# Pairing the small transforms on TensorE, moving a buffer and a store, and sending weights out earlier, in a two-layer convolution and FFN kernel

## The chip, the cores and the metric

The kernel runs on one core of one Trainium2 chip. Its time is the device time of one execution in microseconds (us). Before the change the median of three runs is 916.47 us (916.46 to 917.86). The engines are named as in the profile: PE is TensorE (matrix multiply), DVE is VectorE, ACT is ScalarE, POOL is GpSimd, SP is SyncE, which here only issues DMA transfers. PSUM is the memory that PE writes to; DVE and ACT empty it.

## The reference

Two layers follow each other; each adds a gated long convolution and then a gated FFN to x (2048 tokens, 576 features, 4608 hidden features). All inputs are bf16.

```python
def _A_ref(q, k, v, shift_k, ssm_k, ssm_D):
    ...                                   # k_shift: 4 taps along the tokens
    kv = k_shift * v
    kv_f = rfft(kv padded to 2*S); kf_f = rfft(ssm_k padded to 2*S)
    y = irfft(kv_f * kf_f)[:S]            # causal convolution, by feature
    y = y + kv * ssm_D
    return q * y
def _B_ref(x, w_gate, w_up, w_down):
    return (_gelu(x @ w_gate) * (x @ w_up)) @ w_down
x = A_q
x = x + _A_ref(_layernorm(x), A_k, A_v, A_shift_k, A_ssm_k, A_ssm_D)
x = x + _B_ref(_layernorm(x), B_w_gate, B_w_up, B_w_down)
...                                       # the same two lines once more
```

The convolution of a layer does not depend on x, so its result y serves both layers; only the factor q*y and the FFN follow each other.

## The kernel before, in words

**Tokens and visits.** The tokens are four chunks of 512. A unit is (layer, chunk): in order (0,0), (0,1), (1,0), (1,1), then the same for chunks 2 and 3. The hidden features are split in three phases of 1536. A visit is one unit with one phase; there are 24 visits, 1 to 3 for the first unit, then 4 to 9 for the next two in turn, and so on. Units are numbered from 0, so visit 4 is the first visit of unit 1, which is chunk 1 of layer 0.

**A visit on PE.** First 12 feature tiles (`gu`, line 1047). Each is 18 matmuls: nine steps, in each of which a matmul for w_gate uses rows 0 to 63 of the array and one for w_up rows 64 to 127, at the same time. Their result lies in one PSUM buffer of 2 x 512 columns. Then the down matmuls (`dn`, line 1643), which use all 128 rows: four token blocks of 24 matmuls with 288 columns.

**PSUM.** There are four buffers. One belongs to the convolution (`cps`); three serve feature tiles and down sums in turn (`pr`), so feature tile n+3 can only start when tile n has been read out. In the first visits ("hurry", until the inverse transform of chunk 1 is placed) ACT reads a tile out by a Gelu (line 1614) and a copy (line 1615), and DVE multiplies the two halves (line 1616). Later ACT does the Gelu (line 1624) and DVE multiplies straight out of PSUM (line 1625), so that PSUM is freed by DVE. The scratch tiles `ga` of this have two buffers, which the squares for the layer norm (`junk`, lines 868 and 887) use too.

**The small transforms.** The convolution is made by blocks of 512 tokens from small transforms on PE: for chunk 1 `fwd_eo` (line 299), 8 steps of 4 matmuls for the filter and 8 for kv; for chunks 2 and 3 `quarter` (line 310), 2 matmuls each; and the inverse (line 352), 4 steps of 4 matmuls for each chunk. ACT copies each forward result out of PSUM (`eo`, lines 302 and 312), DVE makes sums and differences from it (`cross`, line 317), and the products follow on DVE. The products of shifted k and v (`kvt`, lines 253 and 259) are DVE's too.

**Rows.** To bring a unit to its FFN: ACT makes the gate factor `yh` (line 921, two buffers), DVE multiplies (line 931), POOL makes the mean, ACT the sum of squares (line 887), POOL the root, DVE the norm (`xn`, line 960). Four such rows of 128 tokens make up a chunk. SP transposes each into `xnT` by two DMA transposes (line 1002); every feature tile of a visit reads all four. `xnT` has two buffers.

**What sets the order.** The program is written out once, engine by engine. A planner (`Pace`) carries estimated clocks for PE, DVE and ACT; `fill` is called after every feature tile and down step and puts in what it reckons to be ready, and `run_p` puts in a small transform. The engines run their lists in order, so a mistaken estimate shows as a wait. Weights are loaded on SP: `weights` issues a load that falls due within 30 us, or within HOLD = 14 us as long as rows are pending. A group of feature weights is three loads (lines 820 to 822).

**Other names in the change.** `hh` is the filter's spectrum for chunk 1, before in two `kc` tiles and a `y` tile (`hh_tiles`). `natural` transposes filter blocks 2 and 3 by DMA and stores them to DRAM (lines 1128 and 1129, both on SP). `conv.alt` lets a small transform borrow one of the three turning PSUM buffers; before, that is so only in the down part of a visit.

Of the kernel before, what the change touches and what calls it, by code (L numbers as in the profile page):

```python
# [17 lines left out]
P = 128  # L18
# [3 lines left out]
RT = BS // P  # L22
# [13 lines left out]
C_HB = 0.345  # L36
C_FOLD = 0.38
LAG = 0.25
AHEAD = 2.0
SLOW, PRESS = 6.0, 22.0  # L40
HOLD, SOON, QUIET, LEAD, FAR = 14.0, 30.0, 10.0, 1.8, 3.6

# [90 lines left out]
class Conv:  # L133
# [8 lines left out]

    def __init__(self, tc, ctx, pace, gwork, A_k, A_v, A_shift_k, A_ssm_k, A_ssm_D, ident, cps, ypool):
# [34 lines left out]
        self.quiet = 0.0  # L178
        self.eo_at = {"eo": deque([0.0] * 2), "yh": deque([0.0] * 2)}
        self.U, self.gwork = deque(), gwork  # L180
# [187 lines left out]

    def hh_tiles(self, kt):
        if kt == 0:  # L370
            for k in (0, 2):
                self.hh[k] = self.kcp.tile([P, 2, self.D], BF16, tag="kc", name="hh")[:]
        else:
            self.y[1] = self.ypool.tile([P, RT, self.D], BF16, tag="y", name="y")
            for k in (1, 3):
                self.hh[k] = self.y[1][:, k - 1:k + 1, :]

    def step(self, m, kv=None, loaded=False):
# [74 lines left out]
        def fwd(kt, s, h):  # L453
            def run():
                if s == 0 and h == 0:
                    for k in (kt, kt + 2):
                        kc[k] = self.kcp.tile([P, 2, D], BF16, tag="kc", name="kc")
                if (kt, s, h) == (1, 0, 0):
                    self.flush(NEVER)
                free, ring = self.eo_free(True)  # L460
# [20 lines left out]
        def fwd_h(kt, s, h):  # L481
            def run():
                if s == 0 and h == 0:
                    self.hh_tiles(kt)
                free, ring = self.eo_free(True)
# [24 lines left out]
        def v(kt, a, part):  # L510
            def run():
# [6 lines left out]
                def fin(when):  # L518
                    if part == 1:
                        if m == 1 and (kt, a) == (2, 0):  # L520
                            mark("early", when)
# [135 lines left out]
        def steps(filt, ready):  # L657
# [7 lines left out]
            for kt in range(2):  # L665
                for s in range(2):
                    for h in range(2):
                        self.Pq.append((lambda now=filt or kt == 0: max(
                            ready(), 0.0 if self.eo_at["eo"] or self.eo_at["yh"] else NEVER,
                            0.0 if now or "early" in at else NEVER), 0.49, (fwd_h if filt else fwd)(kt, s, h)))  # L670
        steps(True, get("h"))
# [26 lines left out]
    def run_v(self, limit):  # L698
# [15 lines left out]
        return True  # L714

    def run_p(self):
        t = self.t
# [3 lines left out]
        self.cur = 0 if self.ps_free[0] <= t.pe else 1  # L721
        if self.cur and ready() <= t.pe and self.ps_free[0] <= t.pe + (0.0 if (1, RT - 1) in self.y_at else 0.3):
            self.cur = 0
            t.pe = max(t.pe, self.ps_free[0])
# [3 lines left out]
        run()  # L728
        t.pe += cost
        return True  # L730

@with_exitstack
def ssm_geglu_kernel(ctx, tc, A_q, A_k, A_v, A_shift_k, A_ssm_k, A_ssm_D, B_x, B_w_gate, B_w_up,
# [39 lines left out]
    def other():  # L773
        b = pr("cps")
        bank_at[taken[0] % 3] = 0.0
        return b

# [10 lines left out]

    bank_at = [0.0] * 3

    def pr(name):
        while late and taken[0] - late[0][1] >= 2:
            add_late()
        taken[0] += 1
        bank_at[taken[0] % 3] = NEVER
        return bank(turn[(taken[0] - 1) % 3], name)
# [10 lines left out]
    work = pool("work", 2)  # L807
    conv = Conv(tc, ctx, t, gwork, A_k, A_v, A_shift_k, A_ssm_k, A_ssm_D, ident,
                lambda *form: bank(turn[3], "cps", *form), ypool)
# [245 lines left out]
    def turn_row(ui, j, xn, when, entry):  # L1055
# [18 lines left out]
        xn_done[ui] = j + 1  # L1074

    conv.alt_at = lambda: bank_at[(taken[0] + 1) % 3]
    early = {}
# [6 lines left out]
    def weights():  # L1084

        while due:
# [15 lines left out]

    def fill(limit, tensor, conv_first):
        weights()
# [17 lines left out]
    nat = []  # L1122

    def natural(b):
# [3 lines left out]
        nc.sync.dma_start_transpose(out=h, in_=A_ssm_k[:, b * BS:(b + 1) * BS])  # L1128
        nc.sync.dma_start(out=conv.hs[b].rearrange("(r p) d -> p r d", p=P), in_=h)

    with tc.manual_schedule():
# [432 lines left out]
        for at, (wb, ph, ui, first, final) in enumerate(visits):  # L1564
# [30 lines left out]
            hT = hpool.tile([P, FP, CH], BF16, tag="hT", name="hT")  # L1595
            free, gone = deque([0.0] * 3), deque([0.0] * 2, maxlen=2)
            conv.alt = None
            for fi in range(FP):
                n, gi = divmod(wb * FP + fi, FG)
                w = wgu[n]  # L1600
                if wb == 0 and fi in early:
                    pair = early.pop(fi)
                    taken[0] += 1
                    gu_half(pair, fi, 1)
                    t.pe = max(t.pe, free.popleft()) + C_GU / 2
                else:
                    pair = pr("gu")
                    gu(pair, w, gi, lambda a: a, xnT)
                    t.pe = max(t.pe, free.popleft()) + C_GU
                while run_late(NEVER):  # L1610
                    pass
                if (hurry() or conv.V and not aq) and t.act <= t.pe + 0.2:
# [5 lines left out]
                    gone.append(t.on_dve(C_HB, there + 0.15) + 0.1)  # L1618
                    free.append(there + 0.1)
                    bank_at[taken[0] % 3] = free[-1]  # L1620
                    lead = FAR
                else:
# [3 lines left out]
                    gone.append(t.on_dve(C_HT, t.on_act(C_GELU, max(t.pe + 0.15, gone[0])) + 0.15) + 0.1)  # L1626
                    free.append(gone[-1])
                    bank_at[taken[0] % 3] = free[-1]
# [5 lines left out]
                fill(t.pe + C_GU + (lead if fi < FP - 2 else LEAD), hurry(), conv.left > 0)  # L1634
            ahead[:] = [t.pe + RT * FP * C_DN, visits[at + 1][2] if at + 1 < len(visits) else None]
            for j in range(RT):
                acc = pr("dn")
                conv.alt = other
                xa = x_c[c][:, j, :]
# [24 lines left out]
                if layer == 1 and end:  # L1664
# [7 lines left out]
                    else:  # L1672
                        conv.store(dst, ob, t.pe + 0.2 + C_EVD + LAG, entry)
                    bank_at[taken[0] % 3] = t.on_dve(C_EVD, t.pe + 0.2) + 0.15
                else:
                    def plus(c=c, j=j, layer=layer, ph=ph, end=end, acc=acc, xa=xa, xh=xh):
# [11 lines left out]
                        if layer == 0 and end:  # L1688
                            vq.extend(prep(units.index((1, c)), j))
                    late.append((t.pe + 0.2, taken[0], plus))  # L1690
        conv.flush(NEVER)
# [50 lines left out]
```

## Time and profile before

| | us |
|---|---|
| median of 3 runs | 916.47 |
| the profiled execution, its own time | 916.75 |
| its span | 915.0 |
| first feature tile starts | 40.29 |
| visit 2 starts | 85.75 |
| visit 3 starts | 121.03 |
| visit 4 starts | 160.91 |
| PE busy | 910.2 |
| DVE busy | 559.1 |
| ACT busy | 364.0 |
| POOL busy | 139.1 |

The profile is of one execution. Its own time is 1.75 us above its span and 0.28 us above the median of the runs. Busy PE time counts a matmul from start to end, and matmuls overlap, so PE's load is better read from the distance between starts. In the lines of the timeline the columns are: start, length, engine, line, operation, what it writes and reads, how many of them; in brackets the idle time before and what ended it.

### The profile page before, as it was taken

The page shows a single profiled execution, that of the slowest core. Times are in us where ns is not written, and L with a number is a line of the kernel's source. Part 1 is how long each engine was busy: PE and PEld are TensorE (multiplying, and loading weights), DVE is VectorE, ACT ScalarE, POOL GpSimd, SP SyncE. Part 2 cuts the span into 40 slices and gives each one's busy share as a digit, 9 for nine tenths or more (in the row PEclk, how much of TensorE's full clock was granted, in tenths as well). Part 3 has the DMA queues.
Part 4 walks back from the last instruction along what each step waited for, and adds up shares of the span by engine and source line. Part 5 has one row for each costly group of instructions (what it writes and reads, how often), then busy time and mean ns, then how long its engine had stood idle before and what let it go on. Part 6 is the DMA issues. An engine that isn't in the chain of part 4 may idle for free.

```text
span 915.0 us, 19143 instructions
## 1 busy us (share of the span) xinstructions
PE 910.2 (99%) x8049; PEld 520.9 (57%) x8049; DVE 559.1 (61%) x1111; ACT 364.0 (40%) x677; POOL 139.1 (15%) x310
## 2 busy tenths in 40 slices
PE   9999999999999999999999999999999999999998
PEld 7746556465565564655655655646646546556555
DVE  8897989644889886568887843553332334433332
ACT  7774437525435366254244233441121224321211
POOL 5422003320113012231023001210000002100000
PEclk9999999999999999999999999999999999999999
DMA  9999996968519503996944700791720820778640
GB/s 238 313 269 197 241 208 106 194 221 156 182 53 232 138 1 42 273 155 165 247 143 94 161 22 27 132 168 50 146 78 2 155 79 14 143 171 179 131 104 27
DMA packets 128635, 129.40 MB, mean 141 GB/s; under 512 B 43298, under 2 KB 120995, under 8 KB 128548
## 3 DMA queue, kind: packets, MB, share of 16 engines
q1 hardware_dynamic: 119666, 93.81, 49.7%
q0 software_dynamic: 8736, 33.77, 12.1%
q8 instruction: 63, 1.03, 0.5%
q10 hardware_dynamic: 146, 0.59, 0.2%
q14 instruction: 24, 0.20, 0.1%
HBM read 106.91 MB, written 11.80 MB: 130 GB/s over the span
## 4 chain that ended last, share of the span: by engine, by line
PE 99%; POOL 0%; ACT 0%; DVE 0%; issue 0%; ACTq 0%
PE gu L1047 61%; PE dn L1643 31%; PE ps L282 1%; PE cps L299 1%; PE cps L310 1%; PE cps L352 1%; PE ps L1268 0%; PE ps L1047 0%; PE ps L1403 0%; POOL rstd L1488 0%; PE ps L1181 0%; PE ps L1239 0%; PE ps L276 0%; ACT yh L1450 0%; PE ps L1297 0%; POOL ve L1487 0%
## 5 line engine op out<-in xcount | busy, mean ns | idle before, releaser
L1047 PE MATMUL gu<-xnT,wgu 64*128 64x512 bf16 x5148 | 561.8, 376 | 0.0
L1047 PEld LDWEIGHTS <-wgu 64*128 64x128 bf16 x5220 | 250.9, 94 | 305.8 <-issue 8.3
L1643 PE MATMUL dn<-wd,hT 128*128 128x288 bf16 x2304 | 292.8, 286 | 0.0
L1643 PEld LDWEIGHTS <-hT 128*128 128x128 bf16 x2304 | 223.6, 98 | 65.4 <-issue 8.1
L1625 DVE TENSOR_TENSOR hT<-ga,gu 128x512 bf16<-128x512 f32 x173 | 118.7, 687 | 177.1 <-ACT ga L1624 176.8
L1624 ACT ACTIVATE ga<-gu 128x512 f32<-128x512 f32 x173 | 103.0, 596 | 311.4 <-PE gu L1047 309.4
L1614 ACT ACTIVATE ga<-gu 128x512 bf16<-128x512 f32 x113 | 67.5, 598 | 164.7 <-PE gu L1047 155.1
L1616 DVE TENSOR_TENSOR hT<-ga 128x512 bf16<-128x512 bf16 x114 | 47.8, 421 | 60.4 <-ACT ga L1615 60.3
L1615 ACT CAST ga<-gu 128x512 bf16<-128x512 f32 x113 | 65.5, 580 | 0.0
L879 POOL TENSOR_SCALAR means<-s 128x1 f32<-128x1 f32 x28 | 8.5, 304 | 230.7 <-DVE x_c L1679 212.1
L1685 DVE SCALAR_TENSOR_TENSOR x_c<-dn,means,x_c 128x576 f32<-128x576 f32 x28 | 22.9, 816 | 30.2 <-PE dn L1643 30.2
L1687 DVE TENSOR_TENSOR x_c<-x_c,dn 128x576 f32<-128x576 f32 x32 | 24.1, 752 | 26.0 <-PE dn L1643 25.7
L895 POOL TENSOR_TENSOR rstd<-ve,neghalf_t 128x1 f32<-128x1 f32 x56 | 33.2, 593 | 4.7
L329 DVE TENSOR_TENSOR prod<-prod 128x576 bf16<-128x576 bf16 x64 | 29.3, 458 | 2.2
L312 ACT ACTIVATE eo<-cps 128x576 f32<-128x576 f32 x32 | 20.6, 654 | 21.2 <-DVE ab L317 7.0
L1666 DVE TENSOR_TENSOR xn<-x_c,dn 128x576 bf16<-128x576 f32 x15 | 11.3, 754 | 27.6 <-PE dn L1643 27.6
L638 DVE TENSOR_TENSOR kc<-ab,cd 128x288 bf16<-128x288 f32 x64 | 25.3, 452 | 0.0
L921 ACT ACTIVATE yh<-y,rstd 128x576 f32<-128x576 bf16 x28 | 21.3, 772 | 8.3 <-DVE x_c L931 6.3
L427 POOL DMA_DIRECT2D kr<-Kd x20 | 11.1, 554 | 85.4 <-DVE prod L328 83.7
L879 POOL TENSOR_SCALAR nm<-s 128x1 f32<-128x1 f32 x28 | 9.0, 320 | 94.2 <-DVE x_c L931 94.1
L887 ACT ACTIVATE junk<-x_c,nm 128x576 bf16<-128x576 f32 x28 | 21.6, 770 | 1.8 <-DVE hT L1625 1.1
L432 POOL DMA_DIRECT2D hr<-Hd x32 | 17.4, 545 | 28.4 <-DVE prod L328 26.4
(179 smaller groups left out, 607.8 us busy)
## 6 DMA issues: line engine op xcount, KB each, us to landing
wgu<-in_B_w_gate_dram SPq DMA_DIRECT2D x45, 576.0 KB, 5.9
wd<-in_B_w_down_dram SPq DMA_DIRECT2D x30, 864.0 KB, 6.9
wgu<-in_B_w_up_dram SPq DMA_DIRECT2D x45, 512.0 KB, 7.7
hr<-Hd POOLq DMA_DIRECT2D x32, 288.0 KB, 6.3
kr<-Kd POOLq DMA_DIRECT2D x24, 288.0 KB, 5.2
Kd<-kc POOLq DMA_DIRECT2D x12, 288.0 KB, 7.2
k<-in_A_k_dram POOLq DMA_DIRECT2D x3, 1008.0 KB, 11.2
wgu<-in_B_w_up_dram SPq DMA_DIRECT2D x45, 64.0 KB, 7.5
```

Of the source, the lines that this page charges most:

```text
L329: nc.vector.tensor_tensor(out=dst[:, cols], in0=pr[:, 0, cols], in1=pr[:, 1, cols], op=ALU.subtract if part == 0 else ALU.add)
L638: nc.vector.tensor_tensor(out=into[k][:, plane, cols], in0=a, in1=b, op=op)
L895: nc.gpsimd.tensor_tensor(out=v["rstd"][:], in0=ve[:], in1=neghalf_t[:, 0:1], op=ALU.pow)
L1047: nc.tensor.matmul(cols(pair[:, s, :]), lhsT=w[r0:r0 + HK, k, gi * P:(gi + 1) * P], rhs=cols(xnT[r0:r0 + HK, blk_of[k], :]), start=(k == 0 ...
L1614: nc.scalar.activation(out=ga[:, 0, :], in_=pair[:, 0, :], func=ACT.Gelu_apprx_tanh)
L1615: nc.scalar.copy(out=ga[:, 1, :], in_=pair[:, 1, :])
L1616: nc.vector.tensor_tensor(out=hT[:, fi, :], in0=ga[:, 0, :], in1=ga[:, 1, :], op=ALU.mult)
L1624: nc.scalar.activation(out=ga[:], in_=pair[:, 0, :], func=ACT.Gelu_apprx_tanh)
L1625: nc.vector.tensor_tensor(out=hT[:, fi, :], in0=ga[:], in1=pair[:, 1, :], op=ALU.mult)
L1643: nc.tensor.matmul(acc[:, h, 0:HW], lhsT=hT[:, fi, j * P:(j + 1) * P], rhs=wd[2 * wb + fi // WT][:, fi % WT, h * HW:(h + 1) * HW], start=( ...
L1685: nc.vector.scalar_tensor_tensor(out=xh, in0=acc[:, :, 0:HW], scalar=m_[:, 0:1], in1=xh, op0=op, op1=ALU.add)
L1687: nc.vector.tensor_tensor(out=xh, in0=xh, in1=acc[:, :, 0:HW], op=ALU.add)
```

## The change

1. A forward or inverse transform may now be placed between feature tiles only if the next one can follow it at once, into a borrowed PSUM buffer (`pair_ready`), or if it has been passed over more than twice; and, until the inverse of chunk 1 is placed, only if DVE is reckoned to run out of work before the feature tiles of the visit end (`dry`, or if the folded sums for chunk 1's inverse are made). `conv.alt` is therefore set between feature tiles too. Among down matmuls transforms go in as before.
2. The planner keeps account of the borrowed buffer (`borrowed`, `was`) and adds 0.2 us for each place with transforms between feature tiles (`C_TURN`).
3. `hh` becomes one tile in the `xnT` buffers; with that the flush of spills and the "early" condition go.
4. The store of filter block 3 moves from SP to POOL and is issued 22 us after its transpose (`NAT`, `puts`).
5. HOLD goes from 14 to 18 us.

```diff
+C_TURN = 0.2
...
+NAT = 22.0
+HOLD, SOON, QUIET, LEAD, FAR = 18.0, 30.0, 10.0, 1.8, 3.6
...
+    def hh_tiles(self):
+        t = self.xtp.tile([P, RT, 2, self.D], BF16, tag="xnT", name="hh")
+        for k in range(RT):
+            self.hh[k] = t[:, k, :, :]
...
+    def dry(self, tiles):
+        t = self.t
+        work = sum(u[1] for u in self.U) + tiles * C_HB
+        for ready, cost, _ in self.V:
+            if ready() > t.pe:
+                break
+            work += cost
+        return max(t.dve, t.pe) + work < t.pe + tiles * C_GU
+
+    def pair_ready(self):
+        t = self.t
+        if not self.Pq or self.Pq[0][0]() > t.pe:
+            return False
+        two = (len(self.Pq) > 1 and self.Pq[1][0]() <= t.pe and len(self.eo_at["eo"]) + len(self.eo_at["yh"]) > 1
+               and self.ps_free[0] <= t.pe + 0.3 and self.alt is not None and self.alt_at() <= t.pe)
+        self.skipped = 0 if two else self.skipped + 1
+        return two or self.skipped > 2
...
     def weights():
-
+        while puts and puts[0][0] <= t.pe:
+            puts.popleft()[1]()
         while due:
...
+        conv.between = between is not None
+        if tensor and between is not None and not ((1 in conv.z_at or conv.dry(between)) and conv.pair_ready()):
+            return
...
-        nc.sync.dma_start(out=conv.hs[b].rearrange("(r p) d -> p r d", p=P), in_=h)
+
+        def put():
+            (nc.sync if b == 2 else nc.gpsimd).dma_start(out=conv.hs[b].rearrange("(r p) d -> p r d", p=P), in_=h)
+        if b == 2:
+            put()
+        else:
+            puts.append((t.pe + NAT, put))
...
-                    t.pe = max(t.pe, free.popleft()) + C_GU
+                    t.pe = max(t.pe, was[0]) + C_GU
...
+                conv.alt = other if hurry() and not early else None
+                before = t.pe
+                fill(t.pe + C_GU + (lead if fi < FP - 2 else LEAD), hurry(), conv.left > 0, FP - 1 - fi)
+                if t.pe > before:
+                    t.pe += C_TURN
```

More of the change, by code (lines that the diff above doesn't have):

```diff
@@ L40 @@
 SLOW, PRESS = 6.0, 22.0
-HOLD, SOON, QUIET, LEAD, FAR = 14.0, 30.0, 10.0, 1.8, 3.6
+NAT = 22.0
+HOLD, SOON, QUIET, LEAD, FAR = 18.0, 30.0, 10.0, 1.8, 3.6
 class Pace:
@@ L133, with __init__ @@
 class Conv:
-    def __init__(self, tc, ctx, pace, gwork, A_k, A_v, A_shift_k, A_ssm_k, A_ssm_D, ident, cps, ypool):
+    def __init__(self, tc, ctx, pace, gwork, xtp, A_k, A_v, A_shift_k, A_ssm_k, A_ssm_D, ident, cps, ypool):
         self.tc, self.nc, self.t = tc, tc.nc, pace
@@ L177, in __init__ @@
         self.ps_free, self.cur, self.alt, self.alt_at = [0.0, 0.0], 0, None, None
-        self.quiet = 0.0
+        self.quiet, self.skipped, self.between = 0.0, 0, False
         self.eo_at = {"eo": deque([0.0] * 2), "yh": deque([0.0] * 2)}
-        self.U, self.gwork = deque(), gwork
+        self.U, self.gwork, self.xtp = deque(), gwork, xtp
         self.kr_free, self.hr_free = [0.0] * 3, [0.0] * 4
@@ L367, in flush @@
             self.spills.popleft()[1]()
[L369 to L376, printed above, removed]
+    def hh_tiles(self):
+        t = self.xtp.tile([P, RT, 2, self.D], BF16, tag="xnT", name="hh")
+        for k in range(RT):
+            self.hh[k] = t[:, k, :, :]
     def step(self, m, kv=None, loaded=False):
@@ L482, in run @@
             def run():
-                if s == 0 and h == 0:
-                    self.hh_tiles(kt)
+                if (kt, s, h) == (0, 0, 0):
+                    self.hh_tiles()
                 free, ring = self.eo_free(True)
@@ L519, in fin @@
                     if part == 1:
-                        if m == 1 and (kt, a) == (2, 0):
-                            mark("early", when)
                         if m == 1:
@@ L667, in steps @@
                     for h in range(2):
-                        self.Pq.append((lambda now=filt or kt == 0: max(
-                            ready(), 0.0 if self.eo_at["eo"] or self.eo_at["yh"] else NEVER,
-                            0.0 if now or "early" in at else NEVER), 0.49, (fwd_h if filt else fwd)(kt, s, h)))
+                        self.Pq.append((lambda: max(
+                            ready(), 0.0 if self.eo_at["eo"] or self.eo_at["yh"] else NEVER), 0.49, (fwd_h if filt else fwd)(kt, s, h)))
         steps(True, get("h"))
@@ L721, in run_p @@
         self.cur = 0 if self.ps_free[0] <= t.pe else 1
-        if self.cur and ready() <= t.pe and self.ps_free[0] <= t.pe + (0.0 if (1, RT - 1) in self.y_at else 0.3):
+        if self.cur and ready() <= t.pe and self.ps_free[0] <= t.pe + (0.3 if self.between else 0.0):
             self.cur = 0
@@ L729, in run_p @@
         t.pe += cost
+        if self.cur:
+            self.borrowed(self.ps_free[1])
         return True
@@ L773, in other @@
     def other():
-        b = pr("cps")
-        bank_at[taken[0] % 3] = 0.0
-        return b
+        return pr("cps")
     def run_late(limit):
@@ L787, in add_late @@
         bank_at[n % 3] = t.on_dve(C_EVD, ready) + 0.15
-    bank_at = [0.0] * 3
+    bank_at, was = [0.0] * 3, [0.0]
     def pr(name):
@@ L794, in pr @@
         taken[0] += 1
+        was[0] = bank_at[taken[0] % 3]
         bank_at[taken[0] % 3] = NEVER
@@ L1074, in turn_row @@
         xn_done[ui] = j + 1
+    conv.borrowed = lambda when: bank_at.__setitem__(taken[0] % 3, when)
     conv.alt_at = lambda: bank_at[(taken[0] + 1) % 3]
@@ L1101, in pressing, with fill @@
                 and t.pe > due_at[0] - PRESS)
-    def fill(limit, tensor, conv_first):
+    def fill(limit, tensor, conv_first, between=None):
         weights()
@@ L1120, in fill @@
                     break
-    nat = []
+    nat, puts = [], deque()
     def natural(b):
@@ L1595, in ssm_geglu_kernel @@
             hT = hpool.tile([P, FP, CH], BF16, tag="hT", name="hT")
[L1596 removed]
+            gone = deque([0.0] * 2, maxlen=2)
             conv.alt = None
@@ L1604, in ssm_geglu_kernel @@
                     gu_half(pair, fi, 1)
-                    t.pe = max(t.pe, free.popleft()) + C_GU / 2
+                    t.pe += C_GU / 2
                 else:
@@ L1618, in ssm_geglu_kernel @@
                     gone.append(t.on_dve(C_HB, there + 0.15) + 0.1)
-                    free.append(there + 0.1)
-                    bank_at[taken[0] % 3] = free[-1]
+                    bank_at[taken[0] % 3] = there + 0.1
                     lead = FAR
@@ L1637, in ssm_geglu_kernel @@
                 acc = pr("dn")
+                mine = taken[0]
                 conv.alt = other
@@ L1689, in plus @@
                             vq.extend(prep(units.index((1, c)), j))
-                    late.append((t.pe + 0.2, taken[0], plus))
+                    late.append((t.pe + 0.2, mine, plus))
         conv.flush(NEVER)
```

10 lines of the change are left out of this document (3 added, 7 removed).

## The prediction

> **What bounds the kernel now.** I read the page first: busy times and the chain of waits that ended last.
>
> ```profile
> PE 910.2 (99%) x8049; PEld 520.9 (57%) x8049; DVE 559.1 (61%) x1111; ACT 364.0 (40%) x677; POOL 139.1 (15%) x310
> PE 99%; POOL 0%; ACT 0%; DVE 0%; issue 0%; ACTq 0%
> ```
>
> PE sets the end, and the view of waits has no wait of PE after the first feature tile (40.29 us; two of 0.17 and 0.07 show only in the distance of starts). So the change can gain only by sparing PE work or gaps between its matmuls, and loses by any new wait of PE. Next the timeline of PE, in visit 3, where the inverse transforms stand singly between feature tiles:
>
> ```profile
> 132.15 2.12 PE L1047 MATMUL gu<-xnT,wgu 64*128 64x512 bf16 x18
> 134.20 0.66 PE L352 MATMUL cps<-yb,V 128*128 128x288 bf16 x4
> 134.79 2.12 PE L1047 MATMUL gu<-xnT,wgu 64*128 64x512 bf16 x18
> ...
> 137.44 9.89 PE L1047 MATMUL gu<-xnT,wgu 64*128 64x512 bf16 x90
> 147.26 2.87 PE L1643 MATMUL dn<-wd,hT 128*128 128x288 bf16 x22
> ```
>
> One tile and one transform take 134.79 - 132.15 = 2.64. A plain tile is 1.94 (five take 9.82, less a switch, over 5). Four matmuls of 288 columns are 4 x 0.1225 = 0.49 (28 down matmuls from 156.40 to 159.83). What is left, 0.21, is the price of going from 64-row to 128-row matmuls and back.
>
> How near the other engines are is in the stretches and timelines. Busy us of PE, PEld, DVE, ACT in a stretch:
>
> ```profile
> 45.00:71.00 26.00, 26.00 (x220) 11.02 (x219) 24.05 (x49) 20.76 (x44) 7.50 (x16) 1.00 1.05 246
> ```
>
> DVE is 92% busy in visit 1's feature tiles. Then the timelines of DVE, ACT and SP as the rows of unit 1 are made, towards visit 4:
>
> ```profile
> 137.10 0.76 DVE L253 TENSOR_TENSOR kvt<-k,skc 128x1152 bf16<-128x1152 bf16 x1
> 138.11 0.81 DVE L931 SCALAR_TENSOR_TENSOR x_c<-x_b,means,yh 128x576 f32<-128x576 bf16 x1
> 140.65 0.68 DVE L1625 TENSOR_TENSOR hT<-ga,gu 128x512 bf16<-128x512 f32 x1
> ```
> ```profile
> 139.60 0.60 ACT L1624 ACTIVATE ga<-gu 128x512 f32<-128x512 f32 x1 [0.36 <-PE gu L1047]
> 140.09 0.77 ACT L921 ACTIVATE yh<-y,rstd 128x576 f32<-128x576 bf16 x1
> ```
> ```profile
> 145.59 12.54 SPq L1002 DMA_TRANSPOSE xnT<-xn  x8
> 158.67 0.63 SPq L820 DMA_DIRECT2D wgu<-in_B_w_gate_dram  x1
> ```
>
> Eight transposes, then weights. The last transpose is issued at 156.87 and lands 3.4 later, at 160.24; visit 4 starts at 160.91. That is only 0.67 of room. Last, a case with weights before a chunk's last row, on SP:
>
> ```profile
> 582.97 0.63 SPq L820 DMA_DIRECT2D wgu<-in_B_w_gate_dram  x1
> 583.65 0.63 SPq L821 DMA_DIRECT2D wgu<-in_B_w_up_dram  x1
> 584.33 0.64 SPq L822 DMA_DIRECT2D wgu<-in_B_w_up_dram  x1
> 585.07 2.61 SPq L1002 DMA_TRANSPOSE xnT<-xn  x2
> ```
> ```profile
> DMA to landing us min/median/max: 2.5/7.0/7.7
> ```
>
> Those two transposes took 7.0 and 7.7 to land, where 2.5 is the least.
>
> **The change part by part.** The sum is made against the profiled execution (span 915.0, time 916.75), 0.28 above the median of the runs.
>
> *Switches.* The built programs have the same matmuls in another order. Before, transforms stand between feature tiles 15 times (11 in visit 1, the last just before the down matmuls, and 4 in visit 3); after, 6 times (4 and 2). Counting changes from 64-row to 128-row matmuls: 38 before, 30 after. 8 x 0.21 = -1.7. Among down matmuls a transform costs no switch. The ends are 0 and -1.7: no more can be saved by this.
>
> *Visit 1, ACT behind.* A pair gives DVE one product (0.33 from start to start), four sums (4 x 0.37) and two kvt operations (0.67 and 0.79): 3.26. The tile, the pair and a switch give it 1.94 + 0.98 + 0.21 = 3.13. After the fourth pair two tiles follow with the same 3.26 against 1.94 each, so DVE falls some 3 behind, of which about 1 is room; the Gelu two tiles on wants a `ga` buffer that a late product holds, so ACT is about 2 late. From there each tile costs ACT 0.49 + 0.47 + 0.76 (Gelu, copy, square) = 1.72 of 1.94, so in four to five tiles it regains 1 and reads out the last tile about 1.2 late. The first `eo` copy after it (0.65) ends 0.38 + 1.2 + 0.49 + 0.47 + 0.65 + 0.05 = 3.2 after the last feature matmul starts; the third transform, which wants that PSUM buffer, is due after 0.31 + 2 x 0.1225 + 0.98 + 6 x 0.1225 = 2.3. So PE waits 1.0. Before, this part has one wait of 0.17 among down matmuls (starts 77.28 and 77.57 against a pitch of 0.12). Ends: 0.2 and 1.5.
>
> The Trainium skill (TensorEngine Tiling (Array Packing), section PSUM Bottleneck) says that packing speeds up TensorE but not the reading out of PSUM, which may then bound. If reading out stayed hidden, switches and this part would come to -1.7; by the page's rule to less than that, and the rows of ACT above, which give -0.7, agree with it.
>
> *Visit 3, a ring of waits.* In the new order ACT's list has two gate factors (line 921) each ahead of a tile's Gelu that is already due. Each needs a `yh` buffer that DVE's gate step (line 931) frees; that step stands behind the previous tile's product. Before, a Gelu stood ahead of such a factor (139.60, then 140.09). One turn: 0.81 (931) + 0.09 + 0.67 (921, start to start) + 0.60 (1624) + 0.03 + 0.60 (1625) = 2.80 against 1.94, so 0.86 of wait; two turns, +1.7. The first hangs on DVE being late by kvt work as at 137.10. Ends: 0.9 and 1.9.
>
> *Rows behind weights (visit 4).* On SP the new order is rows 1 to 3, a group of weights, row 4. PE is at this point later by -1.7 + 1.0 + 1.7 = +1.0, and one square (0.77) more stands ahead of the Gelu that row 1's norm follows. Row 1's transposes: 145.59 + 1.0 + 0.8 = 147.4. Six issues of 1.25 make 7.5, so the weights go out at 154.9. In the three cases in which weights stand just ahead of a chunk's last row, its second transpose landed 11.4, 11.1 and 9.5 after the group's first issue (363.83 to 375.24, 582.97 to 594.08, 780.36 to 789.86), 10.7 on average. So row 4 is there at 165.6. PE is ready at 160.91 + 1.0 = 161.9 and waits 3.7. Lower end: without the square and with 9.5, 1.7; upper: 0.6 later on ACT and 11.4, 5.0.
>
> The Trainium skill (DMA: Bandwidth & Descriptors, section Queues, rings and completion order) says that a DMA engine takes descriptors in ring order, but that completion is not in order of issue. By ring order the sum below stands; if row 4 overtook the weights, it would be 917.5.
>
> *Other weights (HOLD).* For units 3 and 5 the group now goes out ahead of an earlier row, so row 4 is no longer behind it. Those landings (375.24, 594.08) were just in time for visits 10 (378.73) and 16 (594.35): no gain, and no wait seen to lose.
>
> *The store.* SP no longer waits for the transposed load, which lands at 85.48. PE waited for no weights there, so no gain. POOL takes one issue and waits for that landing; its next load came at 95.29 before. Cost 0, hidden by 9 us; with no cover it would delay that load by what the landing is late.
>
> *hh.* Its buffer was last read by PE before 40 us, and unit 1's `xnT` follows it long after its products. 0 either way: the visit-1 wait above is counted with ACT.
>
> Sum: -1.7 + 1.0 + 1.7 + 3.7 = **+4.7**: span 919.7, time 921.4, and against the median 916.47 + 4.7 = **921.2**.
>
> **The rivals.**
>
> - *Row 4 isn't held by the weights.* It lands 2.5 after its last issue (158.1), at 160.7, before PE. Then -1.7 + 1.0 + 1.7 = +1.0: 917.5, not slower beyond the measurement. It decides where the landing is less than 7 after the weights' issue. Against it: three of three cases. For it: at 780.36 it was 9.5.
> - *ACT and DVE keep up.* Neither wait of visits 1 and 3 arises; PE is at visit 4 at 159.2, the weights go out at 152.2 and row 4 lands at 162.9: wait 3.7, sum +2.0: 918.5. For it: before, PE lost but 0.25 in all to such waits. Against: the lists above, added by rows.
> - *Only the switches count.* Neither, and row 4 on time: 914.8. Against it all of the above.
>
> **How the numbers follow.** Chances: forecast 0.69, row 4 not held 0.12, engines keep up 0.10, switches only 0.09. About 0.2% (1.8 us) is what can be told from no change: above 918.3 is slower, below 914.6 faster. The third case lies on the bound, 0.06 slower and 0.04 same; the last is split 0.05 faster, 0.04 same. So slower 0.75, same 0.20, faster 0.05. Range: the forecast's own is 917.6 (all lower ends: -1.7 + 0.2 + 0.9 + 1.7 = +1.1) to 923.2 (all upper: -1.7 + 1.5 + 1.9 + 5.0 = +6.7); with the second and third cases 917.0 to 923.2, which leaves out the last and some tails.
>
> **What would show it.** In the changed kernel: 30 switches of 0.21; a PE gap of about 1 at the third transform among visit 1's down matmuls, on ACT; two of 0.86 in visit 3's feature tiles, on DVE's product; visit 4 starting at about 165.6 after a wait on row 4's transposes, which land 7 to 8 after issue; nothing later. Wrong if row 4 lands some 3 after issue, or if ACT reads out visit 1's last tile at once.

## The result and the profile after

The changed kernel takes 923.46 us (median of 6 runs, 922.74 to 924.12) against 916.47 in the same session (916.46 to 918.76): +7.0 us between the medians, where +4.7 was forecast. By the means of all these runs it is 1.0070 times as long, 95% interval 1.0057 to 1.0083. Its profiled execution took 923.76, with a span of 921.9 against 915.0.

Lines of the changed kernel are 2 to 28 higher than before: `fwd_eo` 299 is now 301 and the `eo` copy 302 is 304, `gu` 1047 is 1061, `dn` 1643 is 1671, the early Gelu and copy 1614 and 1615 are 1639 and 1640 and their product 1616 is 1641, the single Gelu 1624 is 1648, its product 1625 is 1649, the squares 887 are 901, the gate factor 921 is 935, the gate step 931 is 945, the row transposes 1002 are 1016, the weights 820 to 822 are 834 to 836.

The page of the changed kernel, busy times and the chain that ended last:

```profile
PE 910.2 (99%) x8049; PEld 524.0 (57%) x8049; DVE 558.3 (61%) x1111; ACT 362.9 (39%) x676; POOL 141.5 (15%) x311
PE 91%; DVE 5%; ACT 2%; DMA 1%; issue 1%; POOL 1%; SPq 0%; ACTq 0%; DVEq 0%
```

PE's busy time is what it was. The chain is no longer PE's alone. What PE waited for, in us, times, longest:

```profile
PE gu L1061 <- DMA wgu<-in_B_w_up_dram: 4.6, 1, 4.6
PE gu L1061 <- DVE hT L1649: 1.4, 2, 0.7
...
PE cps L301 <- ACT eo L304: 0.9, 1, 0.9
```

These are the three places that were forecast: visit 4, visit 3, visit 1. The first is put down to a weight load, but visit 4 begins with a group that had gone out at 129.58. The wait is for several semaphores; which one counts is settled by the first experiment. The view counts idle time from a modelled end; the distance between starts, less the usual pitch, gives 4.895 - 0.216 = 4.68, twice 0.86, and 1.177 - 0.1225 = 1.05.

Visit 1: PE's timeline at the third transform among the down matmuls, then ACT's ahead of it (`junk` is a square).

```profile
71.29 0.65 PE L301 MATMUL cps<-v,T 128*128 128x288 bf16 x4 [0.89 <-ACT eo L304]
```
```profile
62.70 0.60 ACT L1639 ACTIVATE ga<-gu 128x512 bf16<-128x512 f32 x1 [1.55 <-DVE hT L1641]
...
69.48 0.25 ACT L901 ACTIVATION_READ_ACCUMULATOR junk<-x_b,means 128x1 f32 x1
69.57 0.64 ACT L1639 ACTIVATE ga<-gu 128x512 bf16<-128x512 f32 x1
70.05 0.64 ACT L1640 CAST ga<-gu 128x512 bf16<-128x512 f32 x1
70.51 1.27 ACT L304 ACTIVATE eo<-cps 128x576 f32<-128x576 f32 x2
```

The Gelu at 62.70 waits 1.55 for a late product of DVE. From there a Gelu, a copy and a square take ACT 1.72 for each tile, so it gains little on PE's 1.94. It reads out the last feature tile only after another square, and the first `eo` copy ends 2.9 after the down matmuls began at 68.27.

Visit 3: PE, then ACT, then DVE.

```profile
139.19 2.12 PE L1061 MATMUL gu<-xnT,wgu 64*128 64x512 bf16 x18 [0.69 <-DVE hT L1649]
142.03 6.00 PE L1061 MATMUL gu<-xnT,wgu 64*128 64x512 bf16 x54 [0.71 <-DVE hT L1649]
```
```profile
137.16 0.78 ACT L935 ACTIVATE yh<-y,rstd 128x576 f32<-128x576 bf16 x1 [3.18 <-DVE x_c L945]
137.84 0.58 ACT L1648 ACTIVATE ga<-gu 128x512 f32<-128x512 f32 x1
140.00 0.78 ACT L935 ACTIVATE yh<-y,rstd 128x576 f32<-128x576 bf16 x1 [1.57 <-DVE x_c L945]
```
```profile
138.46 0.69 DVE L1649 TENSOR_TENSOR hT<-ga,gu 128x512 bf16<-128x512 f32 x1 [1.41 <-ACT ga L1648]
139.06 0.81 DVE L945 SCALAR_TENSOR_TENSOR x_c<-x_b,means,yh 128x576 f32<-128x576 bf16 x1
141.29 0.69 DVE L1649 TENSOR_TENSOR hT<-ga,gu 128x512 bf16<-128x512 f32 x1 [1.41 <-ACT ga L1648]
```

The ring can be read off: the factor waits for the gate step (line 945), the Gelu stands behind the factor, the product waits for the Gelu, the next gate step stands behind the product. One turn is 140.00 - 137.16 = 2.84, where a tile takes 1.94.

Visit 4: SP's queue, and how long the second of the last two transposes (159.20) took to land; the trace has no landing of the first.

```profile
147.63 7.81 SPq L1016 DMA_TRANSPOSE xnT<-xn  x6
155.53 0.60 SPq L834 DMA_DIRECT2D wgu<-in_B_w_gate_dram  x1
...
157.93 3.04 SPq L1016 DMA_TRANSPOSE xnT<-xn  x2
```
```profile
DMA to landing us min/median/max: 7.3/7.3/7.3
```

Row 4 is complete at 159.20 + 7.34 = 166.54, 11.0 after the weights' first issue. Up to here the forecast holds. But visit 4 is also longer than before, 37.37 against 35.53, although it has only two transform matmuls (0.245) more. The stretches around its start show why (busy us of PE, PEld, DVE, ACT, POOL, then the granted clock of PE as a share of full speed):

```profile
161.00:166.00 5.00, 0.39 (x6) 0.11 (x3) 2.31 (x7) 0.39 (x2) 2.46 (x5) 0.97 1.28 153
166.00:169.00 3.00, 3.00 (x14) 1.16 (x16) 0.00 (x0) 0.00 (x0) 0.00 (x0) 0.50 1.11 188
169.00:170.00 1.00, 1.00 (x12) 0.47 (x10) 0.00 (x0) 0.21 (x1) 0.00 (x0) 0.96 1.15 222
```

For some 3 us after the wait, PE runs at half clock: a step of two feature matmuls starts every 0.43 us and not every 0.216. No term of the forecast had this.

The balance of the two spans, by distances between starts: switches 8 x 0.21 = -1.7; visit 1 +0.9 (the wait of 1.05 and others of 0.06, less 0.2 of before); visit 3 +1.65; wait at visit 4 +4.7; a second short wait there, on row 4's second transpose, +0.4; half clock +1.2; first feature tile 0.26 sooner, -0.25. The sum is +6.9, which is the difference of the spans. The last item is not the change's: two later runs of before's instruction order started at 40.03 too. From visit 5 on all visits are as long as before.

### The profile page after: what moved, and what is told of

The parts are those of the page before. It is cut to its first block, busy times and chain, and to the rows that moved or that the text cites. A ratio compares the mean times of both kernels' runs of the same rounds, so it can differ in the third digit from the quotient of the medians.

```text
span 921.9 us, 19147 instructions
## 1 busy us (share of the span) xinstructions
PE 910.2 (99%) x8049; PEld 524.0 (57%) x8049; DVE 558.3 (61%) x1111; ACT 362.9 (39%) x676; POOL 141.5 (15%) x311
## 4 chain that ended last, share of the span: by engine, by line
PE 91%; DVE 5%; ACT 2%; DMA 1%; issue 1%; POOL 1%; SPq 0%; ACTq 0%; DVEq 0%
PE gu L1061 56%; PE dn L1671 29%; PE ps L284 1%; DVE kvt L255 1%; DMA wgu<-in_B_w_up_dram 1%; DVE kvt L261 1%; PE cps L312 1%; DVE hh L319 1%; PE ps L1293 0%; ACT junk L901 0%; DVE hT L1649 0%; PE cps L354 0%; DVE hT L1641 0%; ACT ga L1640 0%; PE ps L1428 0%
## 5 line engine op out<-in xcount | busy, mean ns | idle before, releaser
L1061 PEld LDWEIGHTS <-wgu 64*128 64x128 bf16 x5220 | 253.7, 94 | 311.4 <-issue 15.0
L1639 ACT ACTIVATE ga<-gu 128x512 bf16<-128x512 f32 x112 | 67.0, 598 | 165.6 <-PE gu L1061 154.9
L893 POOL TENSOR_SCALAR means<-s 128x1 f32<-128x1 f32 x28 | 10.6, 380 | 224.8 <-DVE x_c L1707 210.6
L1694 DVE TENSOR_TENSOR xn<-x_c,dn 128x576 bf16<-128x576 f32 x15 | 11.3, 753 | 28.4 <-PE dn L1671 28.4
L908 POOL TENSOR_SCALAR ve<-ss 128x1 f32<-128x1 f32 x56 | 14.6, 262 | 55.0 <-ACT junk L901 54.6
```

The source lines that it names most:

```text
L1061: nc.tensor.matmul(cols(pair[:, s, :]), lhsT=w[r0:r0 + HK, k, gi * P:(gi + 1) * P], rhs=cols(xnT[r0:r0 + HK, blk_of[k], :]), start=(k == 0 ...
L1639: nc.scalar.activation(out=ga[:, 0, :], in_=pair[:, 0, :], func=ACT.Gelu_apprx_tanh)
```

## The experiments

The kernel before itself scatters upward: over all runs from 916.46 to 930.01. The last group of experiments is about that. Medians are compared with the time of its many low runs, 916.5.

**Weights behind row 4 again.**

```diff
-HOLD, SOON, QUIET, LEAD, FAR = 18.0, 30.0, 10.0, 1.8, 3.6
+HOLD, SOON, QUIET, LEAD, FAR = 14.0, 30.0, 10.0, 1.8, 3.6
```

> The kernel after with HOLD back at 14. Only SP's order differs: at visit 4 the group of weights goes out behind row 4's two transposes and not ahead of them (unit 5's group goes back too). Theory: visit 4 started 4.7 us late because row 4 stood behind the weights, and TensorE then ran at half clock for some 3 us, which cost another 1.2 (with a second wait of 0.4 on the last transpose). With the order undone row 4 lands before TensorE is through with visit 3's down matmuls, so 923.5 - 4.7 - 0.4 - 1.2 = 917.2, and the granted clock in the first 5 us of visit 4 is 1.0. Rival: row 4 is late for another reason (its norm or its row is made later in the new order, ACT and DVE being behind), then its landing stays near 166 and the time within 1 of 923.5. Rival two: only the wait goes, not the slow pace: 918.4.

917.53 (917.44 to 918.0, 11 runs): 5.9 less than 923.46, and as the prediction's sum has it with row 4 on time (917.5). The span falls by 6.2, to 915.7. SP's timeline of this run, then two stretches of PE (busy, granted clock):

```profile
147.65 11.39 SPq L1016 DMA_TRANSPOSE xnT<-xn  x8
159.14 0.60 SPq L834 DMA_DIRECT2D wgu<-in_B_w_gate_dram  x1
```
```profile
161.00:166.00 5.00, 5.00 (x48) 1.00 1.06 212
166.00:169.00 3.00, 3.00 (x32) 1.00 1.14 202
```

Visit 4 starts at 161.33 and is 35.77 long. The weights that the profile named go out 3.6 later here, and PE doesn't wait at visit 4: so the wait was for row 4. The rows are made at the same time as in the changed kernel (147.65, 147.63), so a late norm was not the cause. The wait, the second wait and the slow pace vanish together, 6.2 of the span's 6.9.

**One gate factor in flight.**

```diff
-            if gates[0] is not g and not (len(gates) > 1 and gates[1] is g and "yh_at" in gates[0]):
+            if gates[0] is not g:
```

> The kernel after, with a gate factor issued only when the one before it has been used (one in flight ahead of its step, not two): in visit 3 one Gelu goes ahead of the factor that stood before it on ACT; PE's order is the same. Theory: the ring of yh, gate step and product makes both waits of visit 3 (0.85 and 0.87 in the trace); with the Gelu first each shrinks, so visit 3 is 0.9 to 1.7 shorter, and as row 4 is late by the weights' order anyway, which is counted from ACT's chain and not from PE's, up to all of it may turn into a longer wait at visit 4: 921.8 to 923.5. Rival: TensorE waits there only because DVE has too much to do (kvt steps and sums), whatever ACT's order; then the waits stay at 1.7 in sum and the time at 923.5.

921.58 (919.17 to 922.0, 6 runs), -1.9; both waits of visit 3 are gone. ACT's timeline in the place where they were:

```profile
137.42 0.78 ACT L935 ACTIVATE yh<-y,rstd 128x576 f32<-128x576 bf16 x1 [1.91 <-DVE x_c L945]
138.10 0.58 ACT L1648 ACTIVATE ga<-gu 128x512 f32<-128x512 f32 x1
138.75 0.78 ACT L935 ACTIVATE yh<-y,rstd 128x576 f32<-128x576 bf16 x1
139.43 0.58 ACT L1648 ACTIVATE ga<-gu 128x512 f32<-128x512 f32 x1
```

In the changed kernel the two factors stand 2.84 apart; here the second follows after 1.33. DVE has the same work, so the rival (DVE simply overloaded) falls. The rows come sooner too (first transposes at 145.05), so the gain is not eaten by a longer wait at visit 4: that is 3.6 here. The clock falls all the same, in five of the six runs; the sixth, 919.17, has it at 1.0 throughout (there is no trace of that run, so its wait is not known).

**TensorE kept busy in the wait.**

```diff
+            if at == 3:
+                keep = conv.cps()
+                for _ in range(16):
+                    nc.tensor.matmul(keep[:, 0, :], lhsT=ident[:], rhs=wgu[9][:, 0, :], start=True, stop=True)
             hT = hpool.tile([P, FP, CH], BF16, tag="hT", name="hT")
```

> The kernel after, with 16 matmuls of 128x512 more on TensorE between visit 3's last down matmul and visit 4's first feature matmul, whose results nothing reads: 16 x 0.216 = 3.5 us of the wait of 4.7 is filled. Theory: the half clock after the wait comes from TensorE having idled, so with the fill the clock stays at 1.0 and the first feature matmuls run 0.216 apart in place of 0.40; visit 4 starts where it did, and the time is 923.5 - 1.2 = 922.3. Rival: the slow pace comes from something else at that moment (the transfers that run then, late operands); then it stays and the time is 923.5. If the matmuls held up the first feature matmul the time would rise above 923.5.

922.01 (921.72 to 923.43, 5 runs). The profiled run is one of the two near 923.4; PE's timeline and stretches:

```profile
161.23 3.62 PE L1623 MATMUL cps<-wgu,ident 128*128 128x512 bf16 x16
166.84 0.39 PE L1061 MATMUL gu<-xnT,wgu 64*128 64x512 bf16 x2 [1.99 <-DMA xnT<-xn]
167.50 2.77 PE L1061 MATMUL gu<-xnT,wgu 64*128 64x512 bf16 x24 [0.27 <-DMA xnT<-xn]
```
```profile
167.00:169.00 2.00, 1.74 (x16) 1.00 1.15 197
```

With only 2.2 of idle time left the granted clock stays at 1.0, and visit 4 takes 36.22 in place of 37.37, as long as without any slow pace but for its second wait of 0.4. So the slow pace comes from the idle stretch and not from the transfers of that moment, which are the same. In this run row 4's transposes went out 1.0 later than in the changed kernel (158.97; an issue of the weights ahead of them took 1.95), which hides the gain; the three runs at 921.7 to 922.0 show it: -1.5 to -1.7, where -1.2 was expected. All five runs have a granted clock of 0.999 or 1.0, where it was 0.998 without the filling.

**A shorter idle time.** The same insertion with four matmuls, in the kernel with one gate factor in flight, where PE waits 3.6.

```diff
+                for _ in range(4):
```

> The kernel with one gate factor in flight (921.58; TensorE idle for 3.6 before visit 4, then at half clock for 3.4 in five of six runs) with four matmuls of 128x512, which nothing reads, ahead of visit 4's first feature matmul: idle time 3.6 - 0.86 = 2.7. Theory: the clock falls only after an idle stretch of somewhat over 3, so it stays at 1.0, and visit 4 is 35.8 to 36.2 long in place of 37.7: 921.6 - 1.6 = 920.0. Rival: an idle time of 2.7 is enough, at least in some runs: then 921.5 and a clock of 0.998 there.

921.20 (919.08 to 921.69, 12 runs): the rival was right. PE's stretches, cut where the granted clock changes (busy us, then granted clock), and below them the stretch of the run with 16 matmuls in which PE was busy least:

```profile
159.27:162.68 3.41, 1.20 (x7) 1.00 1.38 131
162.68:166.09 3.41, 2.89 (x14) 0.50 1.10 198
```
```profile
162.94:166.35 3.41, 1.91 (x9) 1.00 1.25 157
```

An idle time of 2.8 (3.057 between starts less 0.216) halves the clock in this trace. Eleven of the twelve runs have a granted clock of 0.998; only the one at 919.08 kept 1.0. So an idle stretch of over 3 isn't needed. Its length alone doesn't decide either. Within each trace the changes of the granted clock lie whole multiples of 3.413 apart: in three traces it stays full for 157.01, which is 46 of them, and then at half for 3.413 or 6.827. Cut into such stretches, the traces have nine in which the clock was full and fell at the end, and in each PE was busy for at most 1.28; it was busy for at least 1.91 in every one after which the clock stayed full. The first change comes 4.3 to 7.0 after the start, differently in each run, so the same idle time can lie within one stretch or be split between two. That this is why one run in twelve kept its clock is likely, but there is no trace of that run.

**The order of weights by itself, in the kernel before.** One edit, tried in three versions of that kernel, in `spreads`, at the place where a row goes to its transposes.

```diff
             entry[0] = True
+            if (ui, j) == (1, 3):
+                for d in [d for d in due if d[3] == 11]:
+                    due.remove(d)
+                    load_wgu(11)
```

> The kernel before with one edit: the group of weights that went out behind row 4 of unit 1 goes out ahead of it; nothing else changes on any engine. Theory: row 4 lands 10.7 to 11 after the weights' first issue at 153.1, so at 163.9 to 164.1; TensorE is ready at 160.9 and waits 3.0 to 3.2, so 916.5 + 3.1 = 919.6; if the clock halves after this shorter wait too, up to 1.3 more, 920.9. Rival: in the kernel after row 4 was late because of the later norm, and the order alone costs under 1: below 917.5.

931.6 (923.24 to 937.43, 6 runs), far more than either theory said; even the lowest runs are 2.3 above the upper figure. The profiled run waits in visit 4 as expected in kind (4.1, then the half clock, 1.8), but it has lost more before that: PE's waits there include 9.7 and 2.1 for weights in visit 2. SP stood still from 80.4 to 94.6 before the store of filter block 3, whose transposed load took 31.9 to land. The second version has the store moved to GpSimd, the change's own edit (`natural`, `puts`):

> The kernel before with the store on GpSimd, and the group of weights ahead of row 4 of unit 1: the order of weights by itself, without the wait of SyncE that struck visit 2 in the run before. Theory: TensorE ready at 160.9, row 4 there 10.4 to 11 after the weights' first issue at 153.1, so a wait of 2.6 to 3.2: 919.1 to 919.7 at full clock; with the half clock behind it, which came after waits of 3.6 to 4.7 so far and cost 1.2 to 1.8, 920.3 to 921.5. Rival: without the late norm of the kernel after the order costs under 1: below 917.5.

922.78 (922.12 to 931.97, 12 runs): the scatter upward stays, and the lowest runs, too, lie above the forecast. The profiled run (931.97) waits 4.3 at visit 4, and that visit is 2.9 longer than before. The third version has the store on SP again and the transposed load sooner, as in the last group below.

> The kernel before with the transposed load sooner (916.49 with runs within 0.4) and the group of weights ahead of row 4 of unit 1: the price of that order alone, now without the transfers that scatter in visit 2. In the two earlier traces of this order TensorE waited 4.1 and 4.3 at visit 4, and the half clock behind it cost 1.8 and 2.9. Theory: 916.5 + 4.2 + 1.8 = 922.5, at most 1.1 more. Rival, the sum of the prediction: wait of 2.6 to 3.2 and no loss of clock, 919.1 to 919.7.

923.25 (922.36 to 924.02, 12 runs), against 916.49 for the same kernel without the order: +6.8 for this alone. SP's timeline and PE's stretches:

```profile
145.34 8.96 SPq L1002 DMA_TRANSPOSE xnT<-xn  x6
154.41 1.40 SPq L820 DMA_DIRECT2D wgu<-in_B_w_gate_dram  x1
...
157.59 2.56 SPq L1002 DMA_TRANSPOSE xnT<-xn  x2
```
```profile
161.00:165.00 4.00, 0.02 (x2) 0.73 1.23 185
165.00:166.00 1.00, 1.00 (x6) 0.50 1.08 319
166.00:168.00 2.00, 2.00 (x13) 0.50 1.11 384
```

Visit 4 starts at 164.98, and row 4 is complete at 165.34, 10.9 after the weights' first issue, so the landing distance of the forecast (10.7) was nearly right again. But the weights go out at 154.4 and not at 153.1, since the six transposes ahead take 1.49 each here, and the wait is 4.3; the half clock lasts longer than in the changed kernel, into 168 to 170, and with the second wait costs 2.3.

**Both waits undone.** HOLD at 14 and one gate factor in flight, together.

```diff
+HOLD, SOON, QUIET, LEAD, FAR = 14.0, 30.0, 10.0, 1.8, 3.6
...
+            if gates[0] is not g:
```

> The kernel after with two edits at once: HOLD at 14 (weights behind row 4) and one gate factor in flight. Theory: the two waits of visit 3 (1.72 in sum, gone in the trace with one factor) and the late row with the slow pace behind it (6.2) are independent, and with the factors out of the way row 4 goes out some 2.6 earlier (first row transposes at 145.05 in place of 147.65), so no new wait stands at visit 4: 917.5 - 1.8 = 915.7. Rival: TensorE, 1.8 earlier, meets row 4 at visit 4, which would give up to 1 of it back: 916.7.

915.75 (915.68 to 916.01, 12 runs), as the sum of the two had it. PE has one wait left, in visit 1.

**Squares later.** The same, and ACT's squares kept out of the last three feature tiles and the down part of visit 1.

```diff
-        while run_aq(min(limit, t.pe + 2.3)):
+        while not (wb == 0 and (between is None or between < 3)) and run_aq(min(limit, t.pe + 2.3)):
```

> The kernel of both edits, and three squares of ACT moved from the last three feature tiles of visit 1 into visit 2; TensorE's order is the same. Theory: the wait of 1.06 at the third transform among visit 1's down matmuls is ACT being behind by squares; without them ACT has 0.96 of work to a tile of 1.94 and is level at the end, so the wait goes: 915.7 - 1.06 = 914.6, which is what the change would have given by its switches alone (914.8). Rival: DVE's late products hold the Gelus, not the squares; then the wait stays and the time is 915.7.

914.68 (914.62 to 914.96, 12 runs), -1.07 against the step before. The chain of this kernel, and ACT's timeline at the end of visit 1's feature tiles:

```profile
PE 99%; POOL 0%; ACT 0%; DVE 0%; issue 0%; ACTq 0%
```
```profile
67.11 0.64 ACT L1639 ACTIVATE ga<-gu 128x512 bf16<-128x512 f32 x1
67.59 0.63 ACT L1640 CAST ga<-gu 128x512 bf16<-128x512 f32 x1
68.38 0.60 ACT L1639 ACTIVATE ga<-gu 128x512 bf16<-128x512 f32 x1 [0.15 <-DVE prod L327]
68.87 0.58 ACT L1640 CAST ga<-gu 128x512 bf16<-128x512 f32 x1
69.34 1.21 ACT L304 ACTIVATE eo<-cps 128x576 f32<-128x576 f32 x2
```

The first `eo` copy starts 1.2 sooner than in the changed kernel, and the wait is gone. This version beats both kernels: 1.8 below the low runs of before and 8.8 below the changed kernel. By the visits of the two traces, visit 1 is 1.42 shorter than before and visits 3 and 4 together 0.50, which is the eight switches (8 x 0.21 = 1.7) and before's two short waits (0.17 and 0.07). Against all runs of before in that session the ratio is 0.9947, 95% interval 0.9916 to 0.9979.

**Where before's scatter comes from.** First the store alone, moved as the change does it:

```diff
-        nc.sync.dma_start(out=conv.hs[b].rearrange("(r p) d -> p r d", p=P), in_=h)
+        def put():
+            (nc.sync if b == 2 else nc.gpsimd).dma_start(out=conv.hs[b].rearrange("(r p) d -> p r d", p=P), in_=h)
+        if b == 2:
+            put()
+        else:
+            puts.append((t.pe + 22.0, put))
```

> The kernel before with the store alone moved from SyncE to GpSimd, 22 us after the transposed load was issued. Theory: TensorE waits for no weights in visit 2 when the transposed load lands 22 after its issue, so 0: 916.5 to 916.7. But in a run in which that load landed 31.9 after its issue, SyncE stood before the store and TensorE waited 12 us for weights, so the highest runs (before: up to 929) should be gone, all runs within 1 of each other. Rival: GpSimd's loads behind the store are late and cost some 0.5, or the scatter comes from elsewhere and stays.

916.93 (916.54 to 925.36, 12 runs). In the lowest runs the store costs nothing, as the forecast had it, but the scatter stays. In the profiled run (921.78) PE waits once for weights in visit 2; SP had issued them from 74 on, without standing before the store, and they took up to 29.8 to land. Then the transposed load was issued sooner:

```diff
-                if wb == 0 and fi == 2 * FG:
+                if wb == 0 and fi == FG:
                     natural(3)
```

> The kernel before with the second transposed load (and its store) issued four feature tiles sooner, at about 53 and not at 63; nothing else moves. In the traces of before's order GpSimd issues five transfers (hr, kr, two Hd, kr) between 63 and 72, while the load runs; all five then take 17 to 25 to land and the load 22 to 32. In the kernel after one such transfer falls into the load and it lands after 12. Theory: it is this overlap that makes the runs of before scatter upward (to 929): with the load at 53 only two Hd stores fall into it, it lands after 12 to 16, and all runs lie within 1 of 916.5. Rival: the load itself is slow beside the weights, or the scatter arises in visit 2's own transfers: then runs above 919 remain.

916.49 (916.46 to 916.81, 12 runs), where the kernel before, run beside it, lay between 916.48 and 930.01. So the load's place makes the scatter. Time to landing of this load is the last figure of these two lines, before and here (the least is that of the store):

```profile
DMA to landing us min/median/max: 3.7/8.3/22.5
```
```profile
DMA to landing us min/median/max: 3.7/6.9/19.1
```

It isn't the 12 to 16 that was expected, but it now ends at 74.6 in place of 85.5, and of the group of weights that PE reads from about 101 on, which stands behind it on SP, the first part lands at 90.3 and not at 96.2. The same edit in the version of 914.68, where it brings the load among GpSimd's transfers:

> The same edit in the kernel of 914.68 (both waits undone, squares later): the transposed load goes out at about 53 and not at 65. There, GpSimd's six transfers of visit 1 (two Hd, hr, kr, two Hd) stand between 54 and 61, so now they fall into the load. Theory: they take 15 to 25 in place of 6 to 9, the load 18 to 30 in place of 12 to 17, the products that wait for hr and kr come later, and the time rises above 914.7 by 0.5 or more or scatters upward. Rival: the overlap is harmless by itself: hr and kr land within 10 and the time stays at 914.7.

914.67 (914.62 to 915.02, 12 runs): the rival was right. The overlap does slow the transfers (the load takes 24.5, two of GpSimd's stores, Hd, 17 where they took 7 and 8), but PE waits for none of them. So overlap alone doesn't cost. What seems to cost is a load that ends late with the weights of visit 2 behind it: in the three traces in which PE waits for weights in visit 2 it ends at 91.3, 93.4 and 94.6, in all others by 85.5. That the late end is the cause, and not a sign of something slow at that time, wasn't tried by itself. In the changed kernel it is issued at 64.45 and lands after 11.8, with one transfer of GpSimd's (kr) in it and not five. That this is why its own runs don't scatter (922.74 to 924.12) is likely, but which part of the change does it wasn't tried.

## Why the prediction was right, and where it was short

*Switches, -1.7.* Right: 30 are left, and the version without waits is 1.8 below before.

*Visit 1, +1.0.* Right in place, cause and size: 1.05 at the third transform among the down matmuls, +0.9 against before. ACT fell behind by waiting for a late product (1.55 at 62.70), as forecast, and the wait goes when squares are taken out of its list. (The prediction's load of a pair on DVE adds up to 3.27, not 3.26, which changes nothing.)

*Visit 3, +1.7.* Right: two turns of 2.84 (forecast 2.80), 1.72 of wait; it goes when the Gelu stands ahead of the second factor.

*Rows behind weights, +3.7.* Right in its mechanism, too small in size: the wait is 4.7, and visit 4 starts at 165.98 (forecast 165.6). The distance from the weights' first issue to row 4's landing, 10.7, measured 11.0; but the weights went out at 155.5 (forecast 154.9, six issues taking 7.8 and not 7.5), and PE was ready at 161.3 (161.9), for it had started 0.26 sooner and two transform matmuls had moved behind the wait. The Trainium skill (DMA: Bandwidth & Descriptors, section Queues, rings and completion order) has descriptors taken in ring order; the landings of row 4's second transpose here, 6.3 to 7.3 after its issue wherever weights go ahead of it and 3.4 to 3.7 where they don't, agree, and the rival that row 4 overtakes the weights fell.

*The term that was missing.* This is the step of the sum that failed: the forecast let PE go on at full pace after a wait and gave no reason. It ran at half clock for some 3 us, +1.2, and stopped briefly for row 4's second transpose, +0.4. With the wait's 1.0 these are the difference between +4.7 and the +6.9 of the spans (less 0.25 for the sooner start and 0.15 in visits 1 and 3). They put the median 0.3 above the upper end of the range, in which all prices were at their highest but this one did not stand.

*HOLD for units 3 and 5, the store, hh: 0 each.* Right for the first two: visits 10 and 16 are as long as before, and the store alone leaves the low runs where they were (916.54). hh was not tried alone; no wait in the changed kernel stands at it.

*The rivals.* ACT and DVE did not keep up. "Only the switches count", 914.8, is what the kernel gives once the three waits are taken away (914.68). "Row 4 isn't held by the weights", 917.5, is what it gives once the weights go out behind row 4 (917.53).

## What to carry to other kernels

A saving on the engine that bounds a kernel is kept only where the lists of the other engines stay in step: here 1.7 us saved on TensorE brought three new waits, each to be read off the order of one queue (squares ahead of the last read-out, a factor ahead of a due Gelu, weights ahead of a row). When TensorE is always busy, price a wait of some 3 us or more at its length and 1 to 3 us more, for the half clock behind it: in six traces here, waits of 2.8 to 4.7 made the visit behind them 1.6 to 2.9 longer, a short second wait included. On a queue that serves both small urgent transposes and large loads, count from the load's first issue, not from the transpose's own.

## What the runs showed of the hardware that was not expected

TensorE's granted clock changes, in all traces here, only at instants that lie whole multiples of 3.413 us apart. It falls to 0.50 at the end of such a stretch when PE was busy for at most 1.28 us of it (nine cases) and stays at 1.0 when PE was busy for 1.91 or more. It rises again after a slow stretch with 2.88 or more of busy time and stays low after one with 2.41 or less. So a wait of 2.8 at visit 4 halved the clock and one of 2.2 did not; and the slow time is 3.4, or 6.8 where the wait reaches far into the slow stretch (by 1.0 and 2.1 in two of the three traces of the weights' order in the kernel before). With a wait of 3.6 the clock fell 0.4 after matmuls had begun again. The Trainium skill (TensorE: Matmul & The Clock Gate, section Part 1: The HAM clock gate (the "warmup" mystery)) tells of this gate: half rate after an idle window of about 3.4 us, full rate after a busy one. The traces agree on half rate and on the length of the window; but the window need not be wholly idle here, since one with 1.28 us of busy time was enough.

A DMA transpose from DRAM of 128 x 4 x 576 elements takes 9.0 to 10.3 us to land where it goes out at 36, and 11.3 to 31.9 where it goes out between 55 and 66, depending on what runs beside it. With five of GpSimd's transfers issued while it runs (before's order) these take 16.5 to 25, where such transfers take 5 to 9 in the changed kernel's order.
